# One PSUM bank for the second expert layer, and one-row first stores

## The chip, the cores and the metric

The kernel runs on one core of a Trainium2 chip. The metric is the device time of one execution in microseconds (us). A core has five engines with queues of their own: PE (matrix products), ACT and DVE (element work), POOL (here it issues the loads and builds masks) and SP (here it issues the stores). All of them share one on-chip memory and 16 DMA engines. PE writes to PSUM, a memory of 8 banks of 512 fp32 columns on 128 partitions; ACT and DVE empty it ("evict").

## What is computed

```python
scores = q @ k.T / 8                              # 8 batches, 8 heads, 576 tokens, head size 64
attn   = softmax(where(mask, scores, -1e9))       # heads 0-3: window of 32; heads 4-7: window of 128, step 4
x      = (attn @ v) rearranged to (4608, 512)
logits = x @ phi                                  # (4608, 32): 8 experts of 4 slots
slot_input = softmax(logits, over tokens).T @ x
slot_out[e] = maximum(slot_input[e] @ w1[e], 0) @ w2[e]     # 512 -> 1024 -> 512, per expert
out    = softmax(logits, over slots) @ slot_out   # (4608, 512) fp32, 9.4 MB
```

## The kernel before

The attention runs in eight units (two batches and four heads each) and fills most of the execution. While it runs, POOL's queue loads the inputs and then the expert weights: `w1` first, then `w2`. The change lies in what follows, the tail.

**Parts of w2.** `w2` comes in eight loads, in this order: `p3a`, `p0`, `p1`, `p2` hold all 512 output columns of some rows; the last four, `p3b`, `p3c` (columns 0 to 255) and `p3d`, `p3e` (columns 256 to 511), hold half of the columns each. The loop over `parts` (L901) issues the products of one part as soon as it has landed. A product has a stationary operand of 32 columns of `hT`, the hidden layer, and writes 32 partitions of PSUM; four neighbouring products write the four groups of 32 partitions. Before, each product covers 256 columns, so a part with all columns is gone through twice (`h_` 0 and 1), and the accumulator `sp_` is a pair of banks, one for each half of the columns.

**Slot outputs.** Two instructions at L943 or L942 scale the halves of `sp_` by `rcs` into `so_sb`, half 0 as soon as `p3b` and `p3c` are in, half 1 after `p3d` and `p3e`. Half 0 of the output can so be worked on while half 1 of the weights is still under way.

**Output.** The tokens are cut into `TILES` of n rows per partition, (2, 3, 3, 2, 4, 6, 16) before: tile o holds 128 n tokens, n consecutive ones in each partition. For the first `NSPLIT` tiles (10 rows in all) the halves of the columns are done apart: products of 256 columns at L1009, in groups of one, one, two, two, two and two rows, evictions at L997 (DVE) or L996 (ACT), and one store for each tile and half (L969). All other rows are products of 512 columns at L1034, evicted by DVE and ACT in turn, and one store for each tile.

**Order.** `Prog.schedule` plans every engine's order when the program is built. Of the operations that are ready on an engine it takes those whose start is within 0.1 us of the earliest, and of these the one with the smallest `key`; it also gives out PSUM banks. The stores are an exception: SP's queue keeps the order in which the code makes them, half 0 of the split tiles, then half 1, then the other tiles. Products of `p3d` and `p3e` have keys of K1 + 33.9 and K1 + 34.2; the half-0 groups at L1009 have K1 + 30 + tile number + a tenth of the row.

Of the kernel before, what the change touches and what calls it, by code (L numbers as in the profile page):

```python
# [7 lines left out]
AluOp = mybir.AluOpType  # L8
ACTF = mybir.ActivationFunctionType
# [43 lines left out]
class Op:  # L53
    n = 0
# [75 lines left out]
class Prog:  # L130
# [7 lines left out]
    def op(self, e, fn, r=(), w=(), a=(), alloc=(), cost=0.5, key=0.0, mode="f",  # L138
           sem=None, nbytes=0, nd=0, nq=1, ni=2, after=()):
        o = Op(e, fn, cost, key, mode)  # L140
        deps = list(after)
        for b in r:
            deps += b.ready
        for b in w:
            b.fresh()
            deps += b.prev
        for b in a:
            deps += b.prev
        seen = set()
        for d in deps:  # L150
            if d.id not in seen:
                seen.add(d.id)
                o.deps.append(d)
        for b in r:
            b.reads.append(o)
        for b in list(w) + list(a):
            b.ready.append(o)
        o.wr = [b for b in list(w) + list(a) if b.pool is not None]
        for b in list(r) + list(w) + list(a):
            if b.pool is not None and b not in o.touch:  # L160
                b.left += 1
                o.touch.append(b)
        o.alloc = list(alloc)
        o.sems = sem
        o.ni = ni + 2
        o.dma = nbytes / 435e3 + 0.011 * nd / 16 + 0.022 * nq
        self.ops.append(o)
        return o
# [149 lines left out]
def bass_dilated_sliding_attn__then__soft_moe_slots_kernel(  # L318
# [11 lines left out]
    P = Prog()  # L330
    op = P.op

    def sb(name, shape, dt=BF16):
        return A(nc.sbuf_tensor(name, shape, dt))
# [28 lines left out]
    rcs = sb("rcs", [128, 1], F32)  # L363
# [4 lines left out]
    hT = sb("hT", [128, 16, 128])  # L368
    half = sb("half", [128, 2, 16])
    scr = sb("scr", [16, len(TURNS), 2, 8])  # L370
    so_sb = sb("so_sb", [128, DM])
# [4 lines left out]
    psum = Pool(8, {1: [[i] for i in (6, 7, 0, 1, 2, 3, 4, 5)], 2: [[0, 1], [2, 3], [4, 5], [6, 7]]})  # L376
# [8 lines left out]
    def tile(pool, size=1):  # L385
        t = Buf(pool)
        t.size = size
        return t
# [4 lines left out]
    def pair(t):  # L393
        return ps[:, t.phys[0]:t.phys[0] + 2, :]

    def bank(t):
        return ps[:, t.phys[0], :]
# [12 lines left out]
    b_psA, b_csum, b_rcs = [Buf() for _ in range(3)]  # L410
    b_expT, b_expX = [Buf() for _ in range(B)], Buf()
    b_half = Buf()
    b_siT, b_h, b_hT, b_so = Buf(), [Buf(), Buf()], [Buf(), Buf()], [Buf(), Buf()]
# [23 lines left out]
    HOME = {}  # L437
# [59 lines left out]
    lo = 8192  # L497
    for n_ in ("p3c", "p3d", "p3e"):
        hi = lo + 256 * (W2[n_][2] - W2[n_][1])
        home(TTf[:, lo:hi], b_TT, n_)  # L500
        lo = hi
# [3 lines left out]
       w=[b_phist], cost=0.1, sem=s_phi, nbytes=65536)  # L505
# [5 lines left out]
       r=[b_id0], w=[b_id], cost=1.6)  # L511
# [4 lines left out]
    def asel(t, sl, base, pat, cm):  # L516
# [7 lines left out]
       r=[b_mask[0]], w=[b_mask[1]], cost=0.6)  # L524
# [11 lines left out]
    for i, t in enumerate(VNt):  # L536
# [6 lines left out]
       cost=0.1, key=1)  # L543
    op("dve", lambda g: g.memset(half[:], 0.0), w=[b_half], cost=0.1, key=1)
    for x in range(2):
        for j in range(4):
# [3 lines left out]
               r=[b_id], w=[b_half], cost=0.1, key=1)  # L550
    for j in range(4):
        op("dve", lambda g, j=j: g.tensor_copy(fold[32 * j:32 * j + 32, :],
                                               ident[32 * j:32 * j + 32, 32 * j:32 * j + 32]),
           r=[b_id], w=[b_fold], cost=0.1, key=1)
    for j in range(4):
        op("dve", lambda g, j=j: g.tensor_copy(phi_pad[:, :, j, :], phi_st[:]),
           r=[b_phist], **{"w" if j == 0 else "a": [b_phi]}, cost=0.2, key=1)
# [270 lines left out]
    for n_ in ("p3b", "p3c", "p3d", "p3e"):  # L828
        wload(n_)

    K1 = 1000.0
    op("dve", lambda vv: vv.tensor_reduce(rcs[:], csum[:], mybir.AxisListType.X, AluOp.add),
       r=[b_csum], w=[b_rcs], cost=0.1, key=K1)
# [3 lines left out]
    def pe_f(t):  # L837
# [9 lines left out]
        r=[fo], w=[b_siT], cost=0.25, key=K1)  # L847
# [5 lines left out]
    for hh in range(2):  # L853
        def pe(t, hh=hh):
            for c in range(4):
                for hi in range(2):
                    for j in range(4):
                        i_ = t.matmul(pair(hp)[32 * j:32 * j + 32, hh, :], siT[:, 512 * hi + 128 * c + 32 * j:
                                                       512 * hi + 128 * c + 32 * j + 32],
                                      w1v[2 * j + hi][:, c, 512 * hh:512 * hh + 512],  # L860
                                      start=(c == 0 and hi == 0), stop=(c == 3 and hi == 1))
            return i_
        ffn1 = op("pe", pe, r=[b_siT] + w1b, a=[hp], w=[b_hp[hh]], alloc=[hp] if hh == 0 else [],
                  cost=1.8, mode="c", key=K1, ni=64)
        if hh == 0:
            op("act", lambda ac: ac.activation(h_sb[:, 0:512], pair(hp)[:, 0, :], ACTF.Relu),
               r=[b_hp[0], hp], w=[b_h[0]], cost=0.65, key=K1)
        else:
            op("dve", lambda vv: vv.tensor_scalar(h_sb[:, 512:1024], pair(hp)[:, 1, :], 0.0, None,
                                                  op0=AluOp.max),  # L870
               r=[b_hp[1], hp], w=[b_h[1]], cost=0.65, key=K1)
# [17 lines left out]
        op(("act", "dve")[p_], ev, r=[ht], w=[b_hT[p_]], cost=0.45, key=K1 + 0.1 * p_)  # L889

    TILES = []
    NSPLIT = 4
    for n in (2, 3, 3, 2, 4, 6, 16):
        TILES.append((128 * sum(x[1] for x in TILES), n))
    tok = [[expT[:, t0 + j:t0 + j + n * 127 + 1:n] for j in range(n)] for t0, n in TILES]
    rcol = [sum(n for _, n in TILES[:i]) for i in range(len(TILES))]
    sp_ = tile(psum, 2)
    b_sp = [Buf(), Buf()]
    parts = [("p3a", 0, 4), ("p0", 0, 16), ("p1", 0, 16), ("p2", 0, 16),
             ("p3b", 4, 14), ("p3c", 14, 16), ("p3d", 4, 14), ("p3e", 14, 16)]  # L900
    for k_, (name, c0, c1) in enumerate(parts):  # L901
        g, lo, _, f0, f1 = W2[name]
        wv = HOME[name][0].rearrange("p (c f) -> p c f", f=f1 - f0)
        for h_ in range(f0 // 256, f1 // 256):
            def pe(t, k_=k_, name=name, g=g, c0=c0, c1=c1, lo=lo, h_=h_, wv=wv, f0=f0):
                for c in range(c0, c1):
                    j = c % 4
                    i_ = t.matmul(pair(sp_)[32 * j:32 * j + 32, h_, 0:256],
                                  hT[:, c, 24 * g:24 * g + 32],
                                  wv[:, c - lo + (name == "p0" and c > 7), 256 * h_ - f0:256 * h_ - f0 + 256],  # L910
                                  start=(k_ == 0 and c < 4), stop=(k_ > 3 and c >= 12))
                return i_
            last_ = op("pe", pe, r=b_hT + [HOME[name][1]],
                       alloc=[sp_] if k_ == h_ == 0 else [],
                       a=[sp_, b_sp[h_]], cost=0.13 * (c1 - c0) / 4, mode="c",
                       ni=2 * (c1 - c0),
                       key=K1 + 2 + 0.3 * k_ + 0.1 * h_ + (30 if k_ > 5 else 0))
        if k_ == 2:
            mid = last_
        if k_ == 3:  # L920
            third = last_
# [12 lines left out]

    keep(WARM[1], K1 + 3.9, third)

    for h_ in range(2):
        sl = slice(256 * h_, 256 * h_ + 256)

        def cv(en, h_=h_, sl=sl):  # L940
            if en is nc.scalar:
                return en.activation(so_sb[:, sl], pair(sp_)[:, h_, 0:256], ACTF.Copy, scale=rcs[:, 0:1])  # L942
            return en.tensor_scalar(so_sb[:, sl], pair(sp_)[:, h_, 0:256], rcs[:, 0:1], None, op0=AluOp.mult)  # L943
        op("dve" if h_ == 0 else ("dve", "act"), cv, r=[b_sp[h_], b_rcs], w=[b_so[h_]], cost=0.45,
           key=K1 + 20 + 2 * h_)

    for o_ in P.ops[-2:]:
        o_.touch.append(sp_)
        sp_.left += 1

    WDf = WD[:].rearrange("p e x -> p (e x)").bitcast(F32)
    w17f, p0f, p1f = [HOME[x][0].bitcast(F32) for x in ("w17", "p0", "p1")]
    wdh = [f"w1{e}" for e in range(7)]
    STAGE = [(w17f[:, 0:1024], ["w17"]), (p0f[:, 0:1536], ["p0"]), (p0f[:, 1536:3072], ["p0"]),
             (p0f[:, 3072:4096], ["p0"]), (p1f[:, 0:2048], ["p1"]), (WDf[:, 8192:11264], wdh),
             (WDf[:, 0:8192], wdh)]
    ost = [t.rearrange("p (j f) -> p j f", f=512) for t, _ in STAGE]

    def staged(o):
        b = Buf()  # L960
        for x in STAGE[o][1]:
            b.prev = b.prev + HOME[x][1].ready + HOME[x][1].reads
        return b
# [9 lines left out]
    cols = [(rcol[o] + j, tok[o][j]) for o, (_, n) in enumerate(TILES) for j in range(n)]  # L973
    NS = sum(n for _, n in TILES[:NSPLIT])
    b_rt = [Buf(), Buf()]
# [23 lines left out]
    for h_ in range(2):  # L999
        sl = slice(256 * h_, 256 * h_ + 256)  # L1000
        units = [(o, j) for o in range(NSPLIT) for j in range(TILES[o][1])]
        obs = [staged(o) for o in range(NSPLIT)]
        for us in [units[0:1], units[1:2]] + [units[i:i + 2] for i in range(2, len(units), 2)]:
# [3 lines left out]
            def pe(t, us=us, po=po, sl=sl):  # L1007
                for i, (o, j) in enumerate(us):
# [4 lines left out]
                      ni=2 * len(us))  # L1013
            bs = [obs[o] for o in sorted({o for o, _ in us})]

            def ev(en, us=us, po=po, sl=sl):
# [4 lines left out]
               cost=0.47 * len(us), key=kk)  # L1021
# [3 lines left out]
    nev = 0  # L1025
    for o in range(NSPLIT, len(TILES)):
        ob = staged(o)
        k1 = K1 + 50 + o
        for j0 in range(0, TILES[o][1], 2):
# [3 lines left out]
            for j in range(min(2, TILES[o][1] - j0)):  # L1033
                p0 = op("pe", lambda t, o=o, po=po, j=j, j0=j0: t.matmul(  # L1034
                    pair(po)[:, j, :], tok[o][j0 + j], so_sb[:], start=True, stop=True),
                    r=b_so + b_expT, a=[po], w=[b_po[j]], alloc=[po] if j == 0 else [],
                    after=[p0] if j else [], cost=0.22, key=kk + 0.01 * j)
                o_ = op(("dve", "act")[nev % 2], lambda en, o=o, po=po, j=j, j0=j0: scaled(
                    en, ost[o][:, j0 + j, :], pair(po)[:, j, :], rcol[o] + j0 + j),
                    r=[b_po[j], b_rt[1]], a=[ob], after=ob.prev, cost=0.66, key=kk)  # L1040
# [64 lines left out]
```

## Time and profile before

| | |
|---|---|
| median of 9 runs | 177.69 us (177.11 to 180.27) |
| the profiled execution, its own time | 177.69 us |
| its span, first to last instruction | 176.0 us |
| PE, DVE, ACT busy | 74%, 65%, 55% of the span |
| mean granted clock of PE | 0.924 of full speed |
| stores | 11 DMAs, 9.44 MB |

The span is what the profile covers; the 1.7 us between it and the execution's own time lie around it. Times within the profile are us from the start of the span. A row of the timeline gives start, length, engine, source line, operation, what is written from what, shapes, how many instructions were merged and, in brackets, the idle time ahead of them and what ended it. "PEclk" is the clock that PE was granted, as a share of full speed.

### The profile page before, as it was taken

How to read it: one execution, taken by the hardware profiler on the slowest of the kernel's cores; microseconds unless marked ns; L12 is line 12 of the kernel's file. 1: busy time of each engine (PE TensorE's matmuls, PEld its weight loads, DVE VectorE, ACT ScalarE, POOL GpSimd, SP SyncE). 2: the span in 40 equal slices, each digit the busy share in tenths (PEclk: the TensorE clock that was granted, in tenths of full speed). 3: DMA queues.
4: the chain of work that ended last, by engine and by line, in shares of the span. 5: the costliest groups of instructions: out<-in, count | busy, mean ns of one | idle time of the engine just before them, and what ended most of it. 6: DMA issues, size and time to landing. Idle time of an engine off the chain costs nothing.

```text
span 176.0 us, 5769 instructions
## 1 busy us (share of the span) xinstructions
PE 130.5 (74%) x2583; PEld 102.0 (58%) x2588; DVE 113.6 (65%) x263; ACT 96.3 (55%) x146; POOL 45.1 (26%) x85
## 2 busy tenths in 40 slices
PE   0019898599999859999985999977999964698000
PEld 0019686487888658798864888755554832352000
DVE  6850588857987965888986677998431103599200
ACT  2006889367885945898963978784301002399100
POOL 7991808007007004402007901019000000000000
PEclk9999999969999996999999699999999999579855
DMA  5999999999999999999999999999999999989995
GB/s 82 201 220 211 211 222 212 214 217 209 220 211 214 221 205 217 220 207 217 221 205 216 212 218 214 218 212 207 214 216 223 210 189 197 297 270 425 462 477 238
DMA packets 11704, 40.80 MB, mean 232 GB/s; under 512 B 2208, under 2 KB 7840, under 8 KB 7968
## 3 DMA queue, kind: packets, MB, share of 16 engines
q0 software_dynamic: 8032, 30.94, 87.5%
q1 hardware_dynamic: 3648, 9.50, 13.8%
q8 instruction: 20, 0.33, 0.7%
q14 instruction: 4, 0.03, 0.0%
HBM read 61.93 MB, written 9.44 MB: 406 GB/s over the span
## 4 chain that ended last, share of the span: by engine, by line
PE 41%; DMA 21%; DVE 18%; issue 6%; ACT 4%; POOL 3%; POOLq 0%; DVEq 0%
DMA TT<-in_moe_w_dram 16%; PE ps L591 8%; PE ps L586 6%; PE ps L683 5%; PE ps L629 5%; DMA stg<-in_k_dram 5%; PE ps L654 5%; DVE PT L644 4%; DVE WD L997 4%; PE ps L738 4%; PE ps L711 3%; DVE VN L659 3%; DVE XB L694 3%; ACT TT L611 2%; PE ps L769 2%
## 5 line engine op out<-in xcount | busy, mean ns | idle before, releaser
L636 ACT ACTIVATE PT<-ps 128x768 bf16<-128x768 f32 x48 | 36.9, 814 | 7.7 <-PE ps L629 7.4
L611 ACT ACTIVATE TT<-ps 128x864 f32<-128x864 f32 x32 | 28.4, 895 | 19.2 <-PE ps L591 16.4
L694 DVE TENSOR_TENSOR XB<-ps,RV 96x768 bf16<-96x768 f32 x32 | 30.4, 951 | 0.9
L591 PE MATMUL ps<-ident,stg 96*64 96x96 bf16 x576 | 17.8, 225 | 14.6 <-DMA stg<-in_k_dram 12.5
L591 PEld LDWEIGHTS ps<-ident,stg 96*64 96x64 bf16 x576 | 15.7, 124 | 15.9 <-DMA stg<-in_k_dram 12.5
L659 DVE COPY VN<-ps 128x768 bf16<-128x768 bf16 x32 | 17.0, 542 | 10.6 <-PE ps L654 10.6
L629 PE MATMUL ps<-TT 64*128 64x96 bf16 x384 | 16.4, 211 | 4.7 <-issue 2.7
L683 PE MATMUL ps<-VN,PT 128*128 128x65 bf16 x384 | 18.5, 198 | 1.6 <-DVE XB L694 0.6
L430 POOL DMA_DIRECT2D stg<-in_q_dram x16 | 8.8, 549 | 41.2 <-PE ps L591 25.3
L654 PE MATMUL ps<-ident,TT 128*128 128x128 bf16 x192 | 16.6, 229 | 0.6 <-ACT PT L636 0.4
L683 PEld LDWEIGHTS ps<-VN,PT 128*128 128x128 bf16 x384 | 15.3, 101 | 2.9 <-DVE XB L694 0.8
L724 ACT ACTIVATE XT<-ps 128x576 bf16<-128x576 bf16 x22 | 13.7, 653 | 5.1 <-PE ps L711 5.1
L629 PEld LDWEIGHTS ps<-TT 64*128 64x128 bf16 x384 | 10.2, 97 | 8.8 <-issue 2.7
L711 PE MATMUL ps<-ident,XB 96*128 96x96 bf16 x192 | 13.0, 211 | 3.0 <-issue 2.2
L586 PE MATMUL ps<-ident,stg 96*128 96x96 bf16 x288 | 14.8, 206 | 0.3 <-DVE XB L694 0.3
L644 DVE TENSOR_TENSOR PT<-PT,mask_p 128x768 bf16<-128x768 bf16 x24 | 12.8, 551 | 2.9 <-ACT PT L636 2.6
L586 PEld LDWEIGHTS ps<-ident,stg 96*128 96x128 bf16 x288 | 13.2, 98 | 1.3 <-DVE XB L694 0.5
L644 DVE TENSOR_TENSOR PT<-PT,mask_d 128x768 bf16<-128x768 bf16 x24 | 12.9, 546 | 1.3 <-ACT PT L636 1.3
L654 PEld LDWEIGHTS ps<-ident,TT 128*128 128x128 bf16 x192 | 11.8, 102 | 2.8 <-ACT PT L636 0.5
L996 ACT ACTIVATE stg<-ps,rtok 128x256 f32<-128x256 f32 (+1 forms) x12 | 5.5, 508 | 14.2 <-PE ps L1009 14.2
L711 PEld LDWEIGHTS ps<-ident,XB 96*128 96x128 bf16 x192 | 9.8, 101 | 4.5 <-issue 2.5
L738 PE MATMUL ps<-XT,phi_pad 128*128 128x192 bf16 (+1 forms) x64 | 9.6, 296 | 0.2 <-DVE expX L750 0.2
(86 smaller groups left out, 184.4 us busy)
## 6 DMA issues: line engine op xcount, KB each, us to landing
WD<-in_moe_w_dram POOLq DMA_DIRECT2D x7, 1024.0 KB, 31.7
stg<-in_q_dram POOLq DMA_DIRECT2D x16, 288.0 KB, 21.1
stg<-in_v_dram POOLq DMA_DIRECT2D x16, 288.0 KB, 21.8
stg<-in_k_dram POOLq DMA_DIRECT2D x16, 288.0 KB, 22.9
out_dram<-WD SPq DMA_DIRECT2D x1, 4096.0 KB, 11.4
stg<-in_moe_w_dram POOLq DMA_DIRECT2D x4, 512.0 KB, 25.1
stg<-in_moe_w_dram POOLq DMA_DIRECT2D x1, 2048.0 KB, 24.1
TT<-in_moe_w_dram POOLq DMA_DIRECT2D x1, 2048.0 KB, 25.4
```

Of the source, the lines that this page charges most:

```text
L586: i_ = t.transpose(bankb2(pt, a)[:, 96 * kk:96 * kk + 96], two[:, j // 2, c, :], ident[0:96, 0:96])
L591: i_ = t.transpose(bankb2(pt, a)[64 * hx:64 * hx + 64, 96 * kk:96 * kk + 96], src[:, hx, c, :], ident[0:96, 0:96])
L611: return ac.activation(d, sv, ACTF.Copy)
L629: i_ = t.matmul(pair(sc)[:, hx, QB * x:QB * x + QB], win(u, 1, h01, blk_, bpar)[64 * hx:64 * hx + 64], win(u, 0, h01, blk_, bpar)[64 * hx: ...
L636: op("act", lambda ac: ac.activation(sbt(pt)[:, 0:768].rearrange("p (x n) -> p x n", x=2), pair(sc)[:, :, 0:384], ACTF.Exp, scale=SCALE), ...
L644: return dv.tensor_tensor(p_, p_, m.unsqueeze(1).to_broadcast([128, 2, 384]), AluOp.mult)
L654: i_ = t.transpose(bankb(pv)[:, 128 * m:128 * m + 128], win(u, 2, h01, m, bpar), ident[:, :])
L659: op("dve", lambda dv: dv.tensor_copy(sbt(vn)[:, :, :, 0:64], bankb(pv)[:, 0:768].rearrange("p (m x d) -> p m x d", m=6, x=2)), r=[pv], w= ...
L683: i_ = t.matmul(pair(po)[:, bk, 65 * po_:65 * po_ + 65], sbt(pts[i])[:, o_:o_ + 128], sbt(vn)[:, m, half, 0:65], start=True, stop=True)
L694: op("dve", lambda dv: dv.tensor_tensor(sbt(xb)[:].rearrange("p m (x h d) -> p h x m d", x=2, h=2)[:, h01], pv()[:, :, :, 0:64], sbt(rv)[: ...
L711: i_ = t.transpose(bankb(px)[:, QB * m:QB * m + QB], sbt(xb)[:, m, 128 * x:128 * x + 128], ident[0:QB, 0:QB])
L738: i_ = t.matmul(o_, phi_pad[:, c].rearrange("p j i -> p (j i)"), rhs, start=c == 0, stop=c == 3)
```

## The change

The accumulator `sp_` becomes one bank whose columns 0 to 255 and 256 to 511 are the halves. Parts with all columns are multiplied by products of 512 columns, so `p3a`, `p0`, `p1` and `p2` take 52 products in place of 104; `p3b` to `p3e` are as before. The eviction of half 0 is made ahead of the products of `p3d` and `p3e`, and these wait for it. Both evictions are put on DVE. The first tile of two rows becomes two tiles of one row, and `NSPLIT` 5, so that the same ten rows are split; each half then has five stores in place of four, 13 in all. A staging area is added for the extra tile; the other tiles keep their size and places.

```diff
-    NSPLIT = 4
-    for n in (2, 3, 3, 2, 4, 6, 16):
+    NSPLIT = 5
+    for n in (1, 1, 3, 3, 2, 4, 6, 16):
...
-    sp_ = tile(psum, 2)
+    sp_ = tile(psum, 1)
     b_sp = [Buf(), Buf()]
+
+    def slot_out(h_):
+        sl = slice(256 * h_, 256 * h_ + 256)
+
+        def cv(en):
+            if en is nc.scalar:
+                return en.activation(so_sb[:, sl], bank(sp_)[:, sl], ACTF.Copy, scale=rcs[:, 0:1])
+            return en.tensor_scalar(so_sb[:, sl], bank(sp_)[:, sl], rcs[:, 0:1], None, op0=AluOp.mult)
+        o_ = op("dve", cv, r=[b_sp[h_], b_rcs], w=[b_so[h_]], cost=0.45, key=K1 + 20 + 2 * h_)
+        o_.touch.append(sp_)
+        sp_.left += 1
+        return o_
...
-        for h_ in range(f0 // 256, f1 // 256):
...
+        if k_ == 6:
+            first = slot_out(0)
+
+        def pe(t, k_=k_, name=name, g=g, c0=c0, c1=c1, lo=lo, wv=wv, f0=f0, f1=f1):
+            for c in range(c0, c1):
+                j = c % 4
+                i_ = t.matmul(bank(sp_)[32 * j:32 * j + 32, f0:f1], hT[:, c, 24 * g:24 * g + 32],
+                              wv[:, c - lo + (name == "p0" and c > 7), :],
+                              start=(k_ == 0 and c < 4), stop=(k_ > 3 and c >= 12), skip_group_check=True)
+            return i_
+        last_ = op("pe", pe, r=b_hT + [HOME[name][1]], alloc=[sp_] if k_ == 0 else [],
+                   a=[sp_] + b_sp[f0 // 256:f1 // 256], cost=0.13 * (c1 - c0) / 4 * (f1 - f0) / 256, mode="c",
+                   ni=2 * (c1 - c0), after=[first] if k_ > 5 else [],
+                   key=K1 + 2 + 0.3 * k_ + (30 if k_ > 5 else 0))
...
-    for h_ in range(2):
...
-        op("dve" if h_ == 0 else ("dve", "act"), cv, r=[b_sp[h_], b_rcs], w=[b_so[h_]], cost=0.45,
-           key=K1 + 20 + 2 * h_)
...
+    slot_out(1)
...
-    STAGE = [(w17f[:, 0:1024], ["w17"]), (p0f[:, 0:1536], ["p0"]), (p0f[:, 1536:3072], ["p0"]),
+    STAGE = [(w17f[:, 0:512], ["w17"]), (w17f[:, 512:1024], ["w17"]), (p0f[:, 0:1536], ["p0"]), (p0f[:, 1536:3072], ["p0"]),
```

More of the change, by code (lines that the diff above doesn't have):

```diff
@@ L903, in bass_dilated_sliding_attn__then__soft_moe_slots_kernel @@
         wv = HOME[name][0].rearrange("p (c f) -> p c f", f=f1 - f0)
-        for h_ in range(f0 // 256, f1 // 256):
[L905 to L917, printed above, removed]
+        if k_ == 6:
[11 more added lines that the diff above has]
+                   key=K1 + 2 + 0.3 * k_ + (30 if k_ > 5 else 0))
         if k_ == 2:
@@ L935, in bass_dilated_sliding_attn__then__soft_moe_slots_kernel @@
     keep(WARM[1], K1 + 3.9, third)
-    for h_ in range(2):
[L938 to L943, printed above, removed]
-        op("dve" if h_ == 0 else ("dve", "act"), cv, r=[b_sp[h_], b_rcs], w=[b_so[h_]], cost=0.45,
-           key=K1 + 20 + 2 * h_)
-    for o_ in P.ops[-2:]:
-        o_.touch.append(sp_)
-        sp_.left += 1
+    slot_out(1)
     WDf = WD[:].rearrange("p e x -> p (e x)").bitcast(F32)
```

## Prediction

> **What bounds the kernel now.** I read the page's slices first, to find the stage; then the chain that ended last from 140 us, to see what carries the end; then the timeline and the half-microsecond windows of the tail; last the DMA issues. The chain:
>
> ```profile
> 121.72 28.99 DMA TT<-in_moe_w_dram
> ...
> 150.75 1.10 PE ps L908 x11
> ...
> 151.87 0.49 DVE so_sb L943
> ...
> 152.41 2.31 PE ps L1009 x10
> 154.72 0.22 issue
> 154.94 1.07 PE ps L1034 x2
> ...
> 156.04 0.75 DVE stg L997
> 156.79 5.93 DVE WD L997 x9
> 162.72 0.66 DVEq L1075
> 163.38 0.66 DVE WD L997
> ```
>
> The tail starts when the weights are in: `p3d` lets PE start at 150.75 and `p3e` at 151.43 (the timeline's second wait on a load). Half 1 of `so_sb` follows, ten products of 256 columns, the first of 512, and from 155.2 an unbroken row of evictions on DVE and ACT to 164.04. The last store is issued at 164.1 and takes 11.4 us, to 175.5; 0.5 to the span's end, 1.7 outside: 177.69, which is also the median of the runs.
>
> ```profile
> out_dram<-WD SPq DMA_DIRECT2D x1, 4096.0 KB, 11.4
> out_dram<-WD SPq DMA_DIRECT2D x1, 1536.0 KB, 7.0
> out_dram<-stg SPq DMA_DIRECT2D x1, 1024.0 KB, 5.1
> ```
>
> These are the last three stores; the last column is issue to landing. The smallest stores land in 2.4 us at 256 KB, so some 1.8 is fixed, if 0.6 is the data at 430 GB/s. For 4.19 MB that makes 9.75 + 1.8 = 11.5, and 11.4 is measured: the last store hardly waits for the one ahead. But that one (1536 KB, issued 158.84) lands only at 165.85, so its data end near 165.25 if 0.6 of the fixed part comes after them; the last one's can begin at 164.1 + 1.2. So **two chains meet at 165.3**: the evictions, and the DMA engines, which are busy without a hole from 156.0. To gain, the change must shorten both; to lose, it need lengthen one.
>
> ```profile
> 155.00:155.50 0.50, 0.50 (x2) 0.23 (x2) 0.50 (x2) 0.50 (x2) 0.00 (x0) 0.50 1.01 338
> 155.50:156.00 0.50, 0.50 (x3) 0.17 (x2) 0.44 (x1) 0.48 (x2) 0.00 (x0) 0.55 0.12 39
> 156.00:156.50 0.50, 0.50 (x4) 0.25 (x2) 0.46 (x1) 0.50 (x2) 0.00 (x0) 1.00 1.02 336
> ```
>
> The last three columns of these windows are PE's granted clock, the DMA share and GB/s. The stores have a hole of half a microsecond at 155.5; after it they run without one. The clock was half from 149.2 to 155.9, just where half 1 starts.
>
> **What the Trainium skill says.** "TensorE: Matmul & The Clock Gate", Part 1: PE's clock is halved or given back after free-running windows of about 3.4 us, by how busy PE was. The trace agrees: 6.7 us at half clock are two windows, after a stretch (145 to 149) with long waits on loads. "PSUM — Partial Sum Buffer", The four PSUM rules and bank collisions: the first flagged product clears the flags of its whole bank on its 32 partitions, and an engine may not read a bank that PE is writing. That is why one bank needs the full-width `p3a` first and the wait of `p3d` on `first`; no run here shows a collision. "DMA: Bandwidth & Descriptors", Issuing engines are not separate DMA queues: more issues cost the issuing queue's time, while the data share the same engines. Here an issue takes SP 0.53 to 0.76 us:
>
> ```profile
> L969 SPq DMA_DIRECT2D out_dram<-stg x9: 534/611/755, 149.2 to 157.0; - x9
> ```
>
> **Products of 512 columns.**
>
> ```profile
> 137.67 2.15 PE L908 MATMUL ps<-stg,hT 128*32 128x256 bf16 x72
> 143.38 1.06 PE L908 MATMUL ps<-TT,hT 128*32 128x256 bf16 x32 [1.39 <-DMA TT<-in_moe_w_dram]
> 146.70 0.50 PE L908 MATMUL ps<-stg,hT 128*32 128x256 bf16 x10 [1.73 <-DMA stg<-in_moe_w_dram]
> ```
>
> These are `p3a`, `p0`, `p1` (4 + 16 + 16 products, twice), then `p2`, then `p3b`; the bracket is PE's wait for the load. 72 products take 2.15 us, 30 ns each, because four run side by side. The first expert layer (L858) is the nearest row for 512 columns: 64 products between 131.98 and 135.4, 53 ns each. So 36 x 53 = 1.9 us plus some 0.15 of run-out for 2.15, and 16 x 53 = 0.85 plus the same for 1.06: the halved count gains 0.1 to 0.2 us in all, all of it ahead of waits of 1.4 and 1.7 us for loads. What PE does in those waits (row sums, warm-up products) ends at 142.0 and 145.0. Worth **0**. Without that cover it would be worth 0.2 at most. The loads were issued by 123 and depend on none of it.
>
> **One bank, and the new wait.** `p3d` now waits for the eviction of half 0, done at 147.71 + 0.48 = 148.19; `p3d` can't start before 150.75. Cost **0**, with 2.5 us to spare; behind it on PE stand only half 1's products, which need it anyhow. Both evictions ran on DVE before as well, so pinning them changes nothing. The freed bank: the first product of 512 columns needs two neighbouring free banks while six groups of half 1 hold one each. By 154.94 the first two groups are evicted (DVE 153.32, ACT 153.53), two more at about 154.75, so a pair should be free whichever banks the planner picks. If it is not, PE waits for the evictions that end at 155.19: 0 to +0.3; I take 0.
>
> **The order on PE.** The last half-0 group now belongs to tile 4 and has key K1 + 34.0, above `p3d`'s new 33.8. A smaller key wins only between operations that can start within 0.1 us. By the trace the group can start at about 149.5 and `p3d` at 150.75, so it stays ahead. If the planner took them the other way, rows 8 and 9 would be multiplied after `p3d`: about 0.15 us more on PE ahead of half 1 and a store 1 us later: up to +0.2. I take 0.
>
> **Thirteen stores for eleven.** Evictions and groups of the ten rows are the same; only the stores are cut differently. Half 0 before: issues at 149.18, 149.98, 150.65, 151.28. After, with rows 0 and 1 evicted at 149.05 and 149.15: 149.1, 149.65, then 150.2, 150.85 and 151.45, the last three 0.2 late because SP is still busy. Their data ran dry at about 154.3, with 0.3 us to spare ahead of half 1's first store (issue 153.55 + 1.2); 0.1 to 0.2 of that is used. Half 1 before: 153.55, 154.77, 155.36, 156.03, 157.0. After: row 0, evicted by DVE at 153.32, goes out at 153.35, row 1 at 153.9, SP is free at 154.45, and the store of rows 2 to 4 waits, as before, for ACT until 154.75. From there nothing moves, so the hole at 155.5 stays and the run of stores from 156.0 starts where it did. **0**, with 0.3 us of slack on SP. If both one-row issues cost the longest measured 0.755, SP is free at 154.86, 0.1 late, and as SP then issues back to back until 157.6 this stays: 0 to +0.1. Bytes and 1 KB runs are unchanged. Below nothing: `p3e` lands 0.72 us after `p3d`, just as `p3c` after `p3b` with no store about (146.69 and 147.38), so thinner first stores have no more than 0.05 to give back.
>
> **Sum.** 0 on the end; the unknowns' bounds reach from -0.05 (first stores) to +0.3 (bank), +0.2 (order) and +0.1 (SP), hardly all at once. Forecast 177.7, own range 177.3 to 178.2, as medians of runs that spread from 177.1 to 180.3 move by some 0.2 by themselves. About 0.3%, 0.53 us, is what a measurement of this kernel can tell from no change.
>
> **Rivals.**
>
> *The clock window moves, in favour.* Its phase is free, and the change alters PE's pattern between 137 and 145. If PE keeps full clock through 149 to 156: `p3e`'s two products take 0.2 less, DVE's five rows of half 1 run without PE's gaps and the first 512 columns come 0.5 earlier (0.3 at 155.19 and the 0.2 gap before 156.04). Issues at SP follow, so the DMA run moves along by about the same. -0.5 to -0.8, about 177.0. For it: page and trace show that the clock and nothing else slows half 1. Against: PE's work near 145 to 149 is unchanged. Chance 0.25.
>
> *The clock comes back a window late, against.* If fewer products make PE look less busy and half speed lasts until 159.3, products of 512 columns take 0.43 us (154.94 to 155.37) against 0.33 per row for DVE and ACT together. PE then bounds 3.4 us: 8 rows in place of 10.3, so +0.75, and with a late bank or SP as above 178.3 to 178.9. It decides from the point at which PE's share in 152.5 to 155.9 no longer counts as busy. Against it: that share is about nine tenths and its work is not touched. Chance 0.2.
>
> *The change does what it says and shows it:* the first store of half 1 leaves 0.2 earlier and the hole closes, which would give 0.2 at the end. This needs the store of rows 2 to 4 to move as well; its eviction doesn't. It is within the forecast's range.
>
> **How the numbers follow.** No change 0.55 (177.7), faster 0.25 (177.0), slower 0.2 (178.5). The range of 8 in 10 takes in the faster case's middle and the slower case's lower half: 176.9 to 178.5.
>
> **What would show it.** Right: 52 fewer products at the second layer, with the waits for `p2` and `p3b` longer by what they saved; `p3d` at the same distance behind the load; two more SP issues, half 1's first 0.2 earlier, the third still behind ACT; the last eviction some 13.3 us after `p3d`'s first product, and the last store near 11.4. Wrong: the half-clock stretch in another place or length, an idle PE ahead of L1034 that ends with an eviction, an SP queue that reaches the store of rows 2 to 4 after its data, or a last store that takes clearly over 11.4, which would say that the stores ahead had become the bound.

## The result, and the profile after

The changed kernel takes 179.26 us, median of 16 runs (177.71 to 179.84), against 177.70 for the kernel before (53 runs); ratio 1.008, with a 95% interval from 1.0063 to 1.0097. It is slower by 1.4 us by that ratio (the medians alone are 1.6 apart), where no change was forecast. A few executions of a kernel are over 1.5% above its fastest (two of the 53: 180.08 and 180.27 us); the ratios here and below leave them out. Its profiled execution took 179.21 us, its span is 177.5, so 1.7 lie outside as before.

Read in the order of the prediction, the profile after is at first sight that of the kernel before. The chain of work that ended last:

```profile
150.80 0.50 PE L923 MATMUL ps<-TT,hT 128*32 128x256 bf16 x10 [1.19 <-DMA TT<-in_moe_w_dram]
```

```profile
151.51 0.31 PE ps L923 x2
151.82 0.02 issue
151.84 0.49 DVE so_sb L906
...
152.38 1.48 PE ps L1010 x6
...
154.92 1.00 PE ps L1035 x2
155.92 0.02 issue
155.94 0.75 DVE stg L998
156.69 5.93 DVE WD L998 x9
162.62 0.66 DVEq L1076
163.28 0.66 DVE WD L998
```

The first line is from the timeline: `p3d` is multiplied at 150.80 (before: 150.75). The rest is the chain: each station is within 0.1 us of its old place, and the last eviction ends at 163.94, 0.1 **earlier**. SP's stores keep their time too: the last is issued at 164.0 (before: 164.1). From 150 us on, all that PE, DVE, ACT and SP do is done as soon as before. The loss shows only in the DMA issues; the last column is issue to landing:

```profile
out_dram<-WD SPq DMA_DIRECT2D x1, 4096.0 KB, 13.0
out_dram<-WD SPq DMA_DIRECT2D x1, 1536.0 KB, 8.6
out_dram<-stg SPq DMA_DIRECT2D x1, 1024.0 KB, 6.9
```

13.0 for 11.4, 8.6 for 7.0, 6.9 for 5.1: each of the last three stores lands 1.6 to 1.8 us later. The same delay three times does not look like a backlog of bytes, which would grow or shrink. A window near the end (the last columns are clock, DMA share, GB/s), after and then before:

```profile
175.00:175.50 0.50, 0.00 (x0) 0.00 (x0) 0.00 (x0) 0.00 (x0) 0.00 (x0) 0.50 0.16 66
```

```profile
175.00:175.50 0.50, 0.00 (x0) 0.00 (x0) 0.00 (x0) 0.00 (x0) 0.00 (x0) 0.50 0.01 0
```

The data have run out before; after, 66 GB/s for half a microsecond are 33 KB, one packet of the last store, whose rows have 32 KB in each partition. A store counts 16 steps up on its semaphore, one as each DMA engine has done its part, and the trace has the time of every step. For the last store, 15th and 16th step (us from the start of the span):

```
            1st      15th     16th
before    175.16   175.33   175.35
after     175.12   175.31   176.88
```

**One DMA engine of the 16 is 1.6 us late; the other 15 end when they did.** The store before last is the same (15 by 165.60, the last at 167.23), and so is the one ahead of it (161.88 and 163.65). So the engine lost its time near 160 us and did not make it up, as every store of the run that follows gives each engine an equal share. What it did meanwhile shows in the one queue that neither loads nor stores use. The DMA queues between 148 us and the end, after:

```profile
q1 hardware_dynamic: 3152, 9.44, 79.4%
q0 software_dynamic: 889, 0.44, 10.8%
q8 instruction: 1, 0.02, 0.2%
```

and before:

```profile
q1 hardware_dynamic: 3120, 9.44, 79.3%
q0 software_dynamic: 841, 0.41, 10.4%
```

The columns are packets, MB and share of the engines' time. `q8` is the fetch of instructions, one packet of 16 KB. The Trainium skill gives a product's instruction 64 bytes ("TensorE: Matmul & The Clock Gate", Step-by-step: what each phase is for), so that a packet holds 256; the padded runs below agree. Both executions have 20 such packets in all. Before, the last one is at 146.99 us, ahead of every store; after, it is at 159.37 and takes 0.93 us.

Why it would move: if fetches come as the program of PE runs on, one for every 256 instructions, then an instruction taken away ahead of the tail lets the last fetch fall due later. The change takes 52 products, so 104 instructions (each product has a weight load of its own), and with four branches and a wait fewer 109 (counted in the built programs: 5485 before, 5376 after). The last fetch then falls due 109 instructions nearer the end of the program. How far that is in time is not to be had from the count: the experiments below show that a fetch does not come in step with the products.

### The profile page after: what moved, and what is told of

It reads as the page before. It is cut to its first block, busy times and chain, and to the rows that moved or that the text cites. A ratio compares the mean times of both kernels' runs of the same rounds, so it can differ in the third digit from the quotient of the medians.

```text
span 177.5 us, 5665 instructions
## 1 busy us (share of the span) xinstructions
PE 131.5 (74%) x2531; PEld 102.2 (58%) x2536; DVE 113.8 (64%) x263; ACT 96.8 (55%) x146; POOL 45.1 (25%) x85
## 4 chain that ended last, share of the span: by engine, by line
PE 43%; DMA 20%; DVE 11%; ACT 8%; issue 6%; POOL 3%; POOLq 0%; DVEq 0%
DMA TT<-in_moe_w_dram 15%; PE ps L591 10%; PE ps L586 7%; PE ps L683 5%; PE ps L629 5%; PE ps L654 5%; DMA stg<-in_k_dram 5%; DVE WD L998 4%; ACT PT L636 4%; PE ps L738 4%; PE ps L711 3%; DVE XB L694 2%; ACT TT L611 2%; PE ps L769 2%; ACT XT L724 2%
## 5 line engine op out<-in xcount | busy, mean ns | idle before, releaser
L591 PE MATMUL ps<-ident,stg 96*64 96x96 bf16 x576 | 18.4, 231 | 13.7 <-DMA stg<-in_k_dram 12.6
L591 PEld LDWEIGHTS ps<-ident,stg 96*64 96x64 bf16 x576 | 16.4, 129 | 14.9 <-DMA stg<-in_k_dram 12.6
L711 PE MATMUL ps<-ident,XB 96*128 96x96 bf16 x192 | 13.7, 218 | 1.3 <-DVE XB L694 1.1
L711 PEld LDWEIGHTS ps<-ident,XB 96*128 96x128 bf16 x192 | 10.5, 105 | 2.9 <-DVE XB L694 1.4
L692 DVE RECIPROCAL RV<-ps 96x12 f32<-96x12 f32 x32 | 7.2, 224 | 5.0 <-PE ps L683 4.7
```

Of the source, the lines that this page charges most:

```text
L591: i_ = t.transpose(bankb2(pt, a)[64 * hx:64 * hx + 64, 96 * kk:96 * kk + 96], src[:, hx, c, :], ident[0:96, 0:96])
L711: i_ = t.transpose(bankb(px)[:, QB * m:QB * m + QB], sbt(xb)[:, m, 128 * x:128 * x + 128], ident[0:QB, 0:QB])
```

## The experiments

Two theories stood at the start. **F**: the fetch, moved among the stores, makes one engine late, and the last store waits for it. **S**: the two more stores, or something else that the change adds to the tail (one bank, the wait, the order), cost the time. The table gathers the profiled execution of each kernel, next to the timed ratio; "lag" is the 16th step of the last store less the 15th.

| kernel | last fetch, us | lag, us | ratio to before (95%) |
|---|---|---|---|
| before | 147.0 | 0.0 | |
| after | 159.4 | 1.6 | 1.008 (1.0063 to 1.0097) |
| stores alone | 148.6 | 0.0 | 1.0007 (0.9977 to 1.0037) |
| products alone | 154.9 | 0.7 | 1.0106 (1.0054 to 1.0158) |
| before, 147 instructions more | 161.7 | 1.9 | 1.0105 (1.0073 to 1.0137) |
| after, 109 more | 147.0 | 0.0 | 0.9993 (0.9972 to 1.0015) |
| after, 77 more | 147.4 | 0.1 | 1.0000 (0.9979 to 1.0020) |
| after, 41 more | 149.9 | 0.0 | 1.0037 (1.0010 to 1.0064) |
| after, 37 fewer | 163.0 | 1.6 | 1.0165 (1.0108 to 1.0221) |
| before, 17 KB on one engine | 150.0 | 1.1 | 1.0062 (1.0038 to 1.0085) |
| before, 17 KB on 16 engines | 148.9 | 0.0 | 0.9995 (0.9976 to 1.0015) |
| before, 70 KB on one engine | 149.8 | 4.0 | 1.0230 (1.0198 to 1.0262) |

The counts of added instructions are those planned. In the built programs the padding makes one wait needless, so they are one less each (146, 108, 76 and 40), and with fewer warm-up products one more wait is needed (36 fewer for 37). Apart from that, PE's other instructions are the same and in the same order in the four padded programs as without the padding.

**The stores alone.** Tiles, `NSPLIT` and staging of the change, on the kernel before:

```diff
-    NSPLIT = 4
-    for n in (2, 3, 3, 2, 4, 6, 16):
+    NSPLIT = 5
+    for n in (1, 1, 3, 3, 2, 4, 6, 16):
```

> The stores' half of the change alone: tiles (1, 1, 3, 3, 2, 4, 6, 16), five split tiles, 13 stores; second layer as before. Theory F (the 109 missing PE instructions move PE's last instruction fetch, 16 KB on one DMA engine, from 147 us into the run of stores at 159 us, and this engine ends 1.6 us late): PE's instruction count is that of before, so the fetch stays near 147; same as before within 0.2%, last store 11.4 us. Rival S (the two more stores cost the time): 1.008 of before, last store near 13.

Measured: 1.0007, last store 11.5 us. The stores cost nothing that can be seen (within 0.4% by the interval), and the last store's 16 engines end together; S falls for them.

**The products alone.** The changed kernel with the old tiles:

```diff
-    NSPLIT = 5
-    for n in (1, 1, 3, 3, 2, 4, 6, 16):
+    NSPLIT = 4
+    for n in (2, 3, 3, 2, 4, 6, 16):
```

> The products' half alone: one PSUM bank and 512 columns, tiles and stores as before. Theory F: PE's instruction count is that of the changed kernel, so the fetch comes near 159 us and the last store takes near 13 us; 1.007 to 1.009 of before. Rival S: same as before, last store 11.4.

Measured: 1.0106, last store 12.4 us in the profile. The whole loss comes with the products. The fetch fell at 154.9 in this execution, not at 159, though PE has the same instructions in the same order as in the changed kernel (a few read other addresses): the time of a fetch varies between executions. In the first store that met it one engine ended 1.8 us after the other 15, in the last one 0.7: an engine can make up some of it. That it does so where the others have to wait for data, as at the hole near 155.5, fits and is not shown.

**The kernel before, with PE's program made longer.** This leaves the change out and brings only its instruction count, up to a multiple of 256:

```diff
     load_unit(1)
+    pad_ = tile(psum, 1)
+
+    def pad_pe(t):
+        for _ in range(73):
+            i_ = t.matmul(bank(pad_)[:, 0:1], ident[:, :], ident[:, 0:1], start=True, stop=True)
+        return i_
+    op("pe", pad_pe, r=[b_id], w=[pad_], alloc=[pad_], cost=0.06 * 73, ni=0)
```

> The kernel before with 73 products of one column added on PE right after the identity is built, while PE waits for the first input (results unused): 147 more PE instructions with the branch of the added operation, so that together with the 109 that the change removes they make 256, the length of one fetch; order of everything else unchanged. Theory F: one more fetch, at the same place in the tail as in the changed kernel, near 159 us; 1.007 to 1.009 of before, last store near 13 us. Rival S, and any theory by bank, wait or stores: same as before.

Measured: 1.0105. No instruction of the tail differs from the kernel before, yet the last engine is 1.9 us late. First the fetch queue over the whole span (packets, MB, share), then the last two stores:

```profile
q8 instruction: 21, 0.34, 0.7%
...
out_dram<-WD SPq DMA_DIRECT2D x1, 4096.0 KB, 13.3
out_dram<-WD SPq DMA_DIRECT2D x1, 1536.0 KB, 8.9
```

There are 21 fetches for 20, and the added one comes at 161.7; the stores take 13.3 and 8.9 for 11.4 and 7.0.

**The changed kernel, with the count restored.** The same addition, 54 products for 73, on the changed kernel:

> The changed kernel with 54 such products of one column at the start: 109 PE instructions with the branch, the number that the change removed. Theory F: the last fetch goes back to about 147 us, ahead of the stores; same as before or up to 0.2% less, last store 11.4 us. Rival S, and any theory by bank, wait or stores: 1.008 of before still.

Measured: 0.9993. All of the change is still there, with 54 useless products on top, and the loss is gone. Between 149 us and the end the trace has no `q8` line, and the stores are back:

```profile
q1 hardware_dynamic: 3152, 9.44, 82.3%
out_dram<-WD SPq DMA_DIRECT2D x1, 4096.0 KB, 11.9
out_dram<-WD SPq DMA_DIRECT2D x1, 1536.0 KB, 7.5
```

These four together leave nothing above some 0.2% for bank, wait, order or stores to explain.

**Taking still more away.** The planner's warm-up products begin later, `FILL = (128,138)` for `(118,138)`:

> The changed kernel with the warm-up products of the planner beginning at 128 instead of 118 us of its plan: 16 products and 5 branches fewer on PE, 37 instructions in all, so that the program ends ahead of the point where the last fetch is asked for; the order of all else is the same. Theory F: no fetch after 144 us, last store 11.4 us, 0.997 to 1.001 of before: taking more instructions away heals what taking 109 away broke. A theory by bank, wait, stores, or by fewer products cooling PE: 1.008 or more, as there are still fewer products.

Measured: 1.0165, the opposite of what F was said to give. The run does not test what it was built for. Its 37 instructions were not enough: the profile still has a last fetch, at 163.0, and a lag of 1.6 us. And in this profile, without the warm-up products, PE ran at half clock from 124 to 140.5 us (0.50 in every window), through the end of the attention and the first three groups of eight products of the first expert layer. The layer began at 138.24 (before: 131.98; after: 135.29), and PE reached `p2` only at 149.40 (before: 143.38, after a wait for the load; after: 145.21):

```profile
138.24 1.04 PE L858 MATMUL ps<-WD,siT 128*32 128x512 bf16 x7
...
141.01 0.32 PEld L858 LDWEIGHTS ps<-WD,siT 128*32 128x32 bf16 x7
141.22 0.60 PE L858 MATMUL ps<-WD,siT 128*32 128x512 bf16 x7
...
149.40 1.05 PE L923 MATMUL ps<-TT,hT 128*32 128x512 bf16 x16
```

The first and third of these timeline rows are the same seven products, at half clock (1.04 us) and at full (0.60). So two losses add up here: the lag of 1.6 us, and a late PE, by which the other 15 engines too end only at 178.27 (before: 175.33). Whether a program so short that no fetch falls due in the tail would be as quick stays open.

**Counts in between.** 38 products of one column, 77 instructions:

> The changed kernel with 38 products of one column at the start: 77 more PE instructions, 32 fewer than in the kernel before, so that the fetch is asked for about 77 program instructions earlier than in the changed kernel, about where the half-1 products of 256 columns start. Theory F, with the hole in the stores at 155.5 us letting the late engine catch up by 0.5 us: fetch between 149 and 154 us, the last engine 0.3 to 1.1 us behind the others, 1.002 to 1.006 of before. Without catching up: 1.008 as in the changed kernel, wherever the fetch falls in the run of stores.

Measured: 1.0000, fetch at 147.4. My place for it, 149 to 154, was wrong: adding 77 instructions brought it back as far as 109 did. A fetch does not come in step with the products, and why is open. And 20 products, 41 instructions:

> The changed kernel with 20 products of one column at the start, 41 PE instructions more. With 77 more the last fetch came at 147.4 us, with none at 159.4 us. Theory F: wherever the fetch falls decides: at 149 us or before, same as before within 0.2%; after 152 us, the last engine 0.5 to 1.6 us late and 1.003 to 1.009.

Measured: 1.0037, between the two, with runs from 177.55 to 180.22. In the profile the fetch came at 149.9, among the last loads, and no engine was late. A later fetch in the other runs would give the rest, but only one execution has its fetch on record here, so this is not shown.

**Work on one engine, without a fetch.** To see whether the lag is anything of the fetch's own, the kernel before got a load on SP just ahead of the last store, which nobody reads:

```diff
+        if o == 6:
+            xs = DmaSem(nc, "s_extra")
+            s_out.append(xs)
+            op("sp", lambda e: [e.dma_start(TTf.bitcast(F32)[0:17, 0:256], moe_w1[0][0:17, 0:256])],
+               after=[third], cost=0.1, sem=xs, nbytes=17408, key=k1)
         store(o, slice(0, 512), ob, k1)
```

> The kernel before (no fetch among its stores) with one extra load on SP between the last two stores, about 159.2 us: 17 rows of 1 KB, 17 KB in all, into a buffer that nobody reads any more. As 17 has no divisor up to 16 but 1, by the Trainium skill's DMA page one DMA engine carries it. Theory F (what costs is work on one engine in the run of stores, which the last store must wait for): that engine ends 0.6 to 1.6 us after the others, 1.003 to 1.008 of before. Rival T (16 KB more are nothing against 4 MB, and the fetch costs for a reason of its own, in PE): same as before within 0.2%.

Measured: 1.0062, lag 1.1 us. That one engine carried the load shows in the load's own semaphore, which moves at two times only, 159.8 and 167.1 us. Then the same bytes as 16 rows of 272 columns, `[0:16, 0:272]`:

> Control for the run before it: the same 17 KB, issued at the same place, as 16 rows of 1088 bytes, so that all 16 engines carry one row each. Theory F: 1 KB on each engine, 0.04 us by 17 KB at 430 GB/s; same as before within 0.2%, all engines end together. Rival T: also the same.

Measured: 0.9995, no lag; the load's semaphore moves in 16 steps. And 17 rows of 1024 columns:

> As with 17 rows of 1 KB, but 17 rows of 4 KB: 70 KB on one engine. Theory F: one engine carries 4 times as much, at some 27 GB/s (430 over 16) 2.6 us, and ends 2.4 to 4 us late; 1.013 to 1.022 of before. Rival T: 0.2 us at most, 1.001.

Measured: 1.0230, lag 4.0 us; the other 15 engines end at 175.21, about where they did (175.33). The semaphore's steps of the last store in the three, as above:

```
                          1st      15th     16th
17 KB on one engine     175.49   175.67   176.81
17 KB on 16 engines     175.05   175.21   175.23
70 KB on one engine     175.01   175.21   179.18
```

The Trainium skill explains the split in "DMA: Bandwidth & Descriptors", Why a DMA increments its semaphore by 16 and not by 1: rows go to as many engines as divide their number, up to 16, so 17 rows to one; these runs agree. Bytes that are nothing in the sum (17 KB of 9.4 MB) cost 1.1 us when one engine has them all, and nothing when 16 share them.

**A version meant to beat both.** The changed kernel with 54 products at the start and more warm-up in the waits:

```diff
-    WARM = (3, 2)
+    WARM = (6, 7)
...
     keep(WARM[1], K1 + 3.9, third)
+    keep(3, K1 + 34.05, first)
```

> A version meant to beat both: the changed kernel with 54 products of one column at the start (fetch ahead of the stores) and more warm-up products of 512 columns in PE's waits for weights: 6 for 3 ahead of p2, 7 for 2 ahead of p3b, and 3 new ones ahead of p3d, after the last half-0 group. If PE then keeps full clock from 149 to 156 us: half 1 some 0.5 us earlier, 0.996 to 0.999 of before. If the windows are judged otherwise, or the warm-up products delay p3b's or p3d's: 1.000 to 1.004.

Measured: 1.0001 (0.9981 to 1.0020). The fetch is at 147.2, the last engine in step, and PE at full clock from 149 to 156, as meant. But the warm-up products pushed `p2` and `p3b` behind their loads: the first layer began at 135.49, as late as in the profile of the changed kernel (135.29), and `p2` came at 146.1 and `p3b` at 148.7, for 145.2 and 146.8 there. The chain runs through PE, but for one eviction, from 136 to 149, and half 0's first store left at 150.60 for 149.18. No gain. The best of the versions run are on a level with the kernel before.

## Why the prediction was wrong

**Step that failed: "The loads were issued by 123 and depend on none of it" asked only what the products do to the loads.** The products were costed as time on PE, "Worth 0. Without that cover it would be worth 0.2 at most", and the only DMAs looked at were loads and stores. That a product is also two instructions that must be brought in by the same 16 DMA engines was not costed. The page before shows the queue, as `q8 instruction: 20, 0.33, 0.7%`; at 0.7% of the engines' time I passed over it. The kernel's planner even keeps the count: its class `Fetch` takes PE's instructions (`ni`, which the edit halves with the products) in lines of 256, and lets PE enter a line no sooner than `LINE` = 5.0 us after the one before. But it charges a fetch to PE alone and never to the DMA engines, and I passed over that too. The sum's missing term is +1.6 us of lag on one engine (1.6 in the profile after, 1.9 with the count alone), which the runs show as +1.4 us for the change and as nothing (0.9993) when the count is restored.

**What held.** The other steps came out. 512 columns: 36 products in 2.13 us against the 1.9 plus 0.15 forecast, and 16 in 1.05 against 0.85 plus the same; the gain is 0.03 us in all, for 0.1 to 0.2, and off the path. The wait for half 0's eviction, the bank and the order cost 0: `p3d` starts 0.05 after its old time and the last half-0 group stays ahead of it. The stores: 1.0007 when alone, half 1's first issued at 153.33 (forecast 153.35), and one-row issues take SP less than I had bounded, 0.35 and 0.43 us in this row of half 0's two (0.34 and 0.45 for half 1's):

```profile
L970 SPq DMA_DIRECT2D out_dram<-stg x2: 349/390/431, 149.2 to 149.6; - x2
```

The waits for `p2` and `p3b` were to grow by what the products saved. In the profile after, the wait for `p2` was gone and that for `p3b` down to 0.49 us from 1.73, because the attention had ended 3.3 us later in that execution (first expert layer at 135.29 for 131.98; the profiles of the kernel before with an extra load have 134.21 to 136.25); this was hidden by the loads and is no effect of the change that any run shows.

**"Two chains meet at 165.3; to lose, the change need lengthen one"** was the right frame, and is why 1.6 us on one engine of 16 shows almost in full. The DMA chain was taken as one server with a mean rate, though; it is 16 servers that must each finish.

**The rivals.** Two of the prediction's signs of being wrong showed. The half-clock stretch was another: 152.3 to 155.7 in the profile after, for 149.1 to 155.9, and half 1's ten products took 2.32 us as before (2.31), so it changed nothing at the end. And the last store took clearly over 11.4, which was to mean that the stores ahead had become the bound; 15 of its engines were on time. The late end by a half clock lasting to 159.3 did not happen. The early clock did not decide this result, but it occurs by itself. In the profile of the stores alone PE was at full clock from 149 to 156; half 1's ten products took 1.27 us, the last eviction ended at 163.4 for 164.04, and the 15th engine at 174.81 for 175.33, as that rival had it. With 147 instructions more, again at full clock, it was 174.93. But with 70 KB on one engine, also at full clock, half 0's first store left 0.65 us later than before and the 15th engine ended at 175.21; with 17 KB on one engine, 1.26 later and at 175.67. So the clock of the tail moves the evictions by half a microsecond, and the end by up to that, when the run of stores also starts on time. The range reached up to 178.5 by the late clock; the mechanism that came was not in it.

## What to carry to other kernels

When an edit changes the number of instructions of an engine, find that engine's instruction fetches in the trace and ask where the next ones will fall: in a stretch where all DMA engines are busy to the end, one 16 KB fetch can cost more than the instructions saved. A transfer that is spread over all engines ends with the slowest of them, so look at the last step of its semaphore, not at GB/s. Before crediting or blaming an edit of this kind, pad the program by harmless instructions to the old count and measure again.

## What the runs showed of the hardware that had not been expected

- A fetch of 16 KB is one packet of 0.88 to 1.12 us (all fetches of the 13 profiles). In the run of stores at the end it left one engine 1.6 to 1.9 us behind the others (three profiles), and 0.7 where it came at 154.9; why it costs more than its own time is open. 17 KB in rows of 1 KB cost 1.1, 70 KB in rows of 4 KB 4.0.
- With the same instructions of PE in the same order the last fetch came at 147.0, 148.6, 148.9, 149.8 and 150.0 us in five profiles, and in two others, with the change's products, at 154.9 and 159.4. Runs of the changed kernel spread from 177.7 to 179.8 us, but those of the kernel before spread as widely (176.8 to 178.6, and the two above 180), so that nothing shows the fetch to be what spreads them.
